# Query blocks of 256, 256, 512, 512, 512, a token-major second MLP product and a reordered prologue in a transformer block

## The chip, the cores and the metric

The kernel runs on one core of one Trainium2 chip. The metric is device time in microseconds (us) of one execution; the span of a profile, from its first to its last instruction, is about 2 us shorter (1296.0 us for an execution of 1298.07 us). TensorE, ScalarE, VectorE and GpSimd are the engines of that core; the profile calls them PE, ACT, DVE and POOL, and writes PEld for the weight loads of TensorE and SPq for DMA transfers issued by SyncE. All times compared below are of runs in the fast state.

## The reference

Shapes: 2048 tokens, width 1024, 32 heads of 32 that share one key and one value head, MLP width 3584, all bf16.

```python
mod = (silu(c) @ w_mod).reshape(1, 6, 1, -1)          # six vectors of 1024
sa, ca, ga, sb, cb, gb = ...
h = layernorm(x) * (1 + ca) + sa
x = x + ga * attention(h)        # q = h@wq (32 heads), k = h@wk, v = h@wv, softmax, @wo
h = layernorm(x) * (1 + cb) + sb
x = x + gb * (silu(h @ w1) * (h @ w3)) @ w2
```

## The kernel before

The program builds a graph of operations. A list scheduler inside the kernel file then lays out, before anything runs, one fixed instruction order for each engine, using durations that are written in the file. The traces below show instructions starting in that order: a VectorE product whose input is there at 716.4 us starts only when the sum ahead of it on VectorE is done, at 717.05 us. So a number such as `0.115` below changes no instruction at all; it changes only the order in which the instructions stand.

```python
def act_t(n):                       # what the scheduler believes a ScalarE instruction takes
    return n / 1200.0 + 0.115
...
    # in schedule(): the tie-break for VectorE, lower is earlier
            elif e == "dve":
                def key(c):
                    s, n = c
                    p = n.prio
                    if t - n.est > 4.0:
                        p -= 3
                    return (p, n.seq)
...
    BLOCKS = [(i * 512, 512) for i in range(NTB)]     # four blocks of 512 queries
    NU = 10                                           # ring of exponential buffers
    NTR = 5                                           # buffers of partial sums
...
    for bi, (q0, qn) in enumerate(BLOCKS):
        attention(q0, qn)      # scores -> exp -> value product, 8 head groups of 4 heads
        post(q0, qn)           # WO, residual, LN2, W1/W3, gate, W2: runs under the next block's attention
```

In a head group each of 16 key tiles takes one score step on TensorE (four heads side by side on 32-row tiles of the array), two exponentials of 128x1024 on ScalarE, and a share of a value product on TensorE. VectorE adds the exponentials in a tree, four tiles to one, and a product with ones turns the sums into denominators.

```python
                G.add("pe", smm, ..., prio=0, cls="S", mode="S", ...)        # score step
                for h in range(2):
                    G.add("act", ... ACT.Exp ..., dur=act_t(2 * npk * qn), prio=0, ...)
                ...
                    G.add("dve", ... TR[tr] = TR[tr] + U[u] ..., prio=3)       # tree sum, 128x2048
```

The MLP of a finished block fills TensorE between these steps. The gate of each of 28 feature tiles is one tanh on ScalarE and two products on VectorE; the first product frees the PSUM bank of the W1 result.

```python
            G.add("act", ... ACT.Tanh(TS <- PB[g1]) ..., dur=act_t(qn), prio=-1)
            G.add("dve", ... TT <- (TS + 1) * PB[g1] ..., prio=0)              # frees the bank of g1
            G.add("dve", ... HHT[ft] <- TT * PB[g3] ..., prio=0)
        ...
            # second product, feature-major: W2 tile stationary, 512 tokens moving
                return e.matmul(b[...], W2S[:, (d0 + j) % 2, fc, :], HHT[:, fc, 0:qn], ...)
            # then scale by the gate per feature, transpose back to tokens (PE), add to X (DVE)
```

The loads of the prologue, in the order of their issue: four token tiles, 4 MB of modulation weights, key and value weights, one eighth of WQ, four token tiles, the rest of WQ, WO, three modulation tiles, and only then the remaining token tiles.

Of the kernel before, what the change touches and what calls it, by code (L numbers as in the profile page):

```python
# [13 lines left out]
class Node:  # L14
    __slots__ = ("eng", "fn", "dur", "lat", "deps", "prio", "seq", "mode", "acq", "touch",
                 "start", "vis", "pos", "ndeps", "users", "need_inc", "cnt", "dsem", "dval", "nbytes", "est", "cls",
                 "sbanks")
# [8 lines left out]
class Dag:  # L26
# [12 lines left out]
    def add(self, eng, fn, reads=(), writes=(), dur=0.1, lat=0.1, prio=5, mode=None, cls=None,  # L39
            acq=None, groups=(), seq=None, dkey=None, nbytes=0, sbanks=()):  # L40
# [41 lines left out]
        for d in n.deps:  # L82
            d.users.append(n)
        n.dsem = n.dval = None
# [9 lines left out]
    def schedule(self, banks):  # L94
# [8 lines left out]
        for n in self.nodes:  # L103
            n.ndeps = len(n.deps)
            n.est = 0.0
            if n.ndeps == 0:
                ready[n.eng].append(n)
# [28 lines left out]
        while left:  # L136
# [85 lines left out]
            if n.dsem is not None:  # L222
                st = max(dma_free, s + 1.2)
                dma_free = st + n.nbytes / 230e3
                n.vis = dma_free + 0.8
            else:
                n.vis = s + d + n.lat
            for u in n.users:
                u.ndeps -= 1
                if not (e == "pe" and u.eng == "pe"):  # L230
                    u.est = max(u.est, n.vis + SEM_LAT)
# [75 lines left out]
def act_t(n):  # L307
    return n / 1200.0 + 0.115
# [9 lines left out]
def build(nc, x_in, wq_in, wk_in, wv_in, wo_in, w1_in, w3_in, w2_in, c_in, wmod_in, out, S, D, F):  # L318
# [9 lines left out]
    BLOCKS = [(i * 512, 512) for i in range(NTB)]  # L328
    NU = 10
    VB = 8  # L330
    R = 4
    NTR = 5
# [12 lines left out]
    WREG = sb("WREG", [P, 4 * 2048 + 2 * NF * P], BF16)  # L345
# [14 lines left out]
    NM = sb("NM", [P, NT], F32)  # L360
# [7 lines left out]
    O2B = HREG[:, o + 1024:o + 2048].rearrange("p (a s) -> p a s", a=2)  # L368
# [6 lines left out]
    U = UREG[:, 0:NU * 2048].rearrange("p (u g s) -> p u g s", u=NU, g=4)  # L375
    TR = UREG[:, NU * 2048:].rearrange("p (u g s) -> p u g s", u=NTR, g=4)
    WM01 = UREG[:, 0:NC * 2048].rearrange("p (c s) -> p c s", c=NC)
    assert (NU + NTR) * 2048 >= NC * 2048
    W1S = WREG[:, 0:2 * 2048].rearrange("p (a c f) -> p a c f", a=2, c=NC)
    W3S = WREG[:, 2 * 2048:4 * 2048].rearrange("p (a c f) -> p a c f", a=2, c=NC)  # L380
    W2S = WREG[:, 4 * 2048:].rearrange("p (a c f) -> p a c f", a=2, c=NF)
    WQ = WREG[:, 4 * 2048 - 2048:4 * 2048 - 2048 + NC * D].rearrange("p (c f) -> p c f", c=NC)
    WMS = WREG[:, 0:6144].rearrange("p (a c f) -> p a c f", a=3, c=4)
    GAB = WREG[:, 4 * 2048 - 2048 + NC * D:4 * 2048 - 2048 + NC * D + 1024]

    SP = nc.alloc_psum_tensor("SP", [P, 3, 2, 512], F32)
    PB = [nc.alloc_psum_tensor("PB%d" % i, [P, 512], F32)[:] for i in range(2)]
    PB += [SP[:, b, h, :] for b in range(3) for h in range(2)]
# [13 lines left out]
    def dma(fn, key, reads=(), writes=(), nbytes=0, prio=5, seq=None):  # L402
        return G.add("sp", fn, reads=reads, writes=writes, dur=0.06, dkey=key, nbytes=nbytes, prio=prio, seq=seq)
# [3 lines left out]
    def xload(t0, n):  # L407
        for t in range(t0, t0 + n):
            dma(lambda e, t=t: e.dma_start(X[:, t % NXS, :], x2[t * P:(t + 1) * P, :]),
                ("x", t % NXS), writes=[("X", t % NXS)], nbytes=P * D * 2)  # L410

    xload(0, 4)
    for k in range(NC):
# [7 lines left out]
    xload(4, 4)  # L421
    dma(lambda e: e.dma_start(WQ[:, :, P:D], wq_in[:, P:D].rearrange("(c p) f -> p c f", p=P)), "wq1",
        writes=[("WQ", 1)], nbytes=7 * P * D * 2)
    dma(lambda e: e.dma_start(WO[:], wo_in.rearrange("(c p) f -> p c f", p=P)), "wo", writes=["WO"], nbytes=D * D * 2)
# [41 lines left out]
    def ln_scale(t0, n):  # L466
        ks = [("MV", t0 + i) for i in range(n)]
        rk = [("RS", t0 + i) for i in range(n)]
        G.add("pool", lambda e: e.tensor_scalar(RS[:, t0:t0 + n], MV[:, t0:t0 + n, 1], EPS, None, ALU.add),
              reads=ks, writes=rk, dur=0.3)  # L470
        G.add("pool", lambda e: e.tensor_tensor(RS[:, t0:t0 + n], RS[:, t0:t0 + n], NHALF[:, 0:n], ALU.pow),
              reads=rk + ["NHALF"], writes=rk, dur=0.4)
        G.add("pool", lambda e: e.tensor_tensor(NM[:, t0:t0 + n], RS[:, t0:t0 + n], MV[:, t0:t0 + n, 0], ALU.mult),
              reads=rk + ks, writes=[("NM", t0 + i) for i in range(n)], dur=0.3)

    def ln_norm(t, q):
        s = t % NXS
        G.add("dve", lambda e: e.tensor_scalar(XN[:, q, :], X[:, s, :], RS[:, t:t + 1], NM[:, t:t + 1],
                                               ALU.mult, ALU.subtract),
              reads=[("X", s), ("RS", t), ("NM", t)], writes=[("XN", q)], dur=0.5, prio=2)  # L480

    def ln_transpose(nt, q0, dst, dkeys, fs, fm, engs, prio=5):
# [3 lines left out]
        for cb in range(NC // ncb):  # L486
            g = grp()
            for i in range(nt):
                def tr(e, i=i, g=g, cb=cb):
                    for h in range(ncb):  # L490
                        c = cb * ncb + h
                        r = e.transpose(PBH[g.bank][:, h * w + i * P:h * w + (i + 1) * P],
                                        XN[:, q0 + i, c * P:(c + 1) * P], IDENT[:])
                    return r
                G.add("pe", tr, reads=[("XN", q0 + i), "IDENT"], dur=ncb * 0.065, lat=0.2,
                      acq=g if i == 0 else None, groups=[(g, "w")], mode="F", prio=prio)
            for h in range(ncb):
                c = cb * ncb + h
                en = engs[cb % len(engs)]
                if en == "act":  # L500
# [4 lines left out]
                        dur=act_t(w) + 0.19, prio=2)  # L505
# [49 lines left out]
    for tb in range(NTB):  # L555
        for i in range(4):
            ln_stats(tb * 4 + i)
        ln_scale(tb * 4, 4)
        for i in range(4):
            ln_norm(tb * 4 + i, i)  # L560
        if tb + 2 < NTB:
            xload(tb * 4 + 8, 4)
        ln_transpose(4, 0, lambda c, tb=tb: HT[:, c, tb * 512:(tb + 1) * 512],
                     lambda c, tb=tb: [("HT", c, tb)], 0, 1, ("act", "dve") if tb == 0 else ("dve",))
        kv(tb)
        if tb == 0:
            qproj(0, 0)
    for f in range(1, NC):
# [5 lines left out]
    nwm = 0  # L574
    GAK = [("GAB",)]
    for h in range(2):
        g = grp()
        for kb in range(2):
            sl = nwm % 3
            nwm += 1  # L580
            dma(lambda e, kb=kb, h=h, sl=sl: e.dma_start(
                WMS[:, sl], wmod_in[kb * 512:(kb + 1) * 512, 2 * D + h * 512:2 * D + (h + 1) * 512]
                .rearrange("(c p) f -> p c f", p=P)), ("wms", sl), writes=wms(sl), nbytes=P * 2048 * 2)
# [314 lines left out]
```

## Time and profile before

The median is 1310.71 us in the runs made first, and 1311.88 us (1310.08 to 1313.36) over all four runs that the result compares (the first three among them).

| stage of the kernel before | from to (us) | what fills it |
|---|---|---|
| prologue and first head group | 0 to 91 | loads, LN1, projections; ScalarE partly idle |
| rest of block 0, two head groups of block 1 | 91 to 384 | attention and q projections, no MLP yet |
| rest of blocks 1 to 3 | 384 to 1107 | attention with MLP beneath it, mostly 33.0 us per head group |
| tail | 1107 to 1309 | TensorE alone: rest of an MLP, then the last MLP |

From the page of the kernel before: busy time of each engine, then 40 equal slices of the span with the busy share, or the granted TensorE clock, in tenths.

```profile
PE 1138.8 (87%) x8561; PEld 439.4 (34%) x8689; DVE 958.9 (73%) x1206; ACT 1015.3 (78%) x1142; POOL 17.1 (1%) x35
...
PE   5387896455779999999899999999999999999998
...
ACT  1368988999999999999979999998999998011100
...
PEclk8688996666889999999999999999999999999999
```

ScalarE has a hole near the start (the 3 in slice 2) and nothing to do in the last six slices. TensorE has slack up to slice 12, where the clock is also low; from there both are full. The average over the span hides that. Busy time of matmuls also overstates them: the Trainium skill, "Trainium Kernel Development and Optimization", section "Performance Expectations", calls it a bad metric because matmuls are pipelined. This trace agrees: one 512-column matmul counts 381 ns in the table of groups, while in a dense stream they start 216 ns apart. The counts and start-to-start times are used below.

Two groups of the page of before: busy time and mean of one in ns, then the idle time before them with its largest releaser.

```profile
L656 ACT ACTIVATE UREG<-SP 128x1024 bf16<-128x1024 f32 x1024 | 968.5, 1067 | 85.5 <-PE SP L646 65.9
...
L646 PE MATMUL SP<-QT,KT 32*128 32x512 bf16 x2048 | 215.4, 411 | 100.0 <-ACT UREG L656 93.9
```

Exponentials and score steps wait for each other. The waits of ScalarE between 29 and 1107 us in the kernel before (total us, times, longest us) are shown below. They include the first head group; from 91 us on the first line is 25.8 us, so ScalarE waits in these two ways for about 42 us in the thousand that follow:

```profile
ACT UREG L656 <- PE SP L646: 65.9, 50, 24.6
ACT UREG L656 <- PE PB L670: 16.6, 8, 3.9
```

One single wait is 24.6 us. The timeline of before (start, length, engine, line, operation, count, and in brackets the idle time before it with its releaser) shows where it comes from:

```profile
20.41 0.88 SPq L424 DMA_DIRECT2D WO<-in_A_wo_dram  x1
21.33 10.25 SPq L581 DMA_DIRECT2D WREG<-in_w_mod_dram  x3
31.70 39.35 SPq L409 DMA_DIRECT2D X<-in_A_x_dram  x16
...
50.47 1.28 DVE L461 BATCH_NORM_STATS2 ST<-X 128x6 f32<-128x512 bf16 x2
...
73.86 2.86 ACT L656 ACTIVATE UREG<-SP 128x1024 bf16<-128x1024 f32 x3 [24.64 <-PE SP L646]
```

The second half of the tokens is asked for at 31.7 us, behind WO and modulation weights; the statistics of the next token tiles can start only at 50.5 us; the exponentials that need their keys start at 73.9 us.

The windows of before: start, end and length, then busy time and instruction count of PE, PEld, DVE, ACT and POOL, granted clock, DMA share, GB/s.

```profile
29.00:91.00 62.00, 35.22 (x339) 17.68 (x339) 45.25 (x81) 29.68 (x32) 3.44 (x8) 0.72 0.36 124
205.00:385.00 180.00, 105.00 (x886) 29.41 (x891) 125.59 (x143) 165.37 (x179) 2.62 (x3) 0.70 0.10 23
1106.70:1155.20 48.50, 48.13 (x291) 23.10 (x295) 28.47 (x50) 1.02 (x2) 1.47 (x3) 1.00 0.48 94
1155.20:1252.20 97.00, 96.53 (x445) 44.08 (x453) 39.02 (x57) 16.72 (x28) 0.00 (x0) 1.00 0.54 151
1252.20:1308.60 56.40, 50.19 (x252) 23.41 (x255) 10.07 (x17) 0.00 (x0) 0.00 (x0) 0.98 0.56 117
```

The first head group needs 62 us with 29.7 us of ScalarE work. From 205 to 385 us TensorE is busy for 58% and the granted clock averages 0.70. The Trainium skill, "TensorE: Matmul & The Clock Gate", section "Part 1: The HAM clock gate", says that the array runs at half clock until it has been busy for a while and falls back when idle; a mean between a half and one in a stretch with idle gaps fits that, and the clock records of the two traces hold only the values 0.5 and 1.0. The last three windows are the tail: 48.5 us until the first W1 matmul of the last MLP, 97.0 us of W1 and W3, 56.4 us of W2 and the stores. TensorE is dense in it.

### The profile page before, as it was taken

What the parts mean: (1) busy time and instruction counts of PE and PEld (TensorE: products, weight loads), DVE (VectorE), ACT (ScalarE), POOL (GpSimd) and SP (SyncE); (2) the same over time, 40 slices, a digit from 0 to 9 for tenths busy, and PEclk for the clock granted to TensorE, in tenths of its full rate; (3) what the DMA queues carried; (4) which work ended last, traced back from release to release, by engine and by line L of the source; (5) the groups of instructions that cost most, each with busy time, mean ns of one, the idle gap of its engine ahead of it and who ended that gap; (6) DMA issues with size and microseconds to landing.
All of it is one profiled execution on the core that took longest, in us unless ns stands there. A gap on an engine that the chain in (4) does not pass through costs nothing.

```text
span 1308.6 us, 21172 instructions
## 1 busy us (share of the span) xinstructions
PE 1138.8 (87%) x8561; PEld 439.4 (34%) x8689; DVE 958.9 (73%) x1206; ACT 1015.3 (78%) x1142; POOL 17.1 (1%) x35
## 2 busy tenths in 40 slices
PE   5387896455779999999899999999999999999998
PEld 3133331111223333333333333333333333444443
DVE  5768786666798888778978887789888887643421
ACT  1368988999999999999979999998999998011100
POOL 1000000000000000000000000000000000000000
PEclk8688996666889999999999999999999999999999
DMA  9415104000003333342423333441533334375545
GB/s 313 151 41 178 33 1 110 12 1 1 1 1 97 98 97 97 94 85 57 120 78 94 95 94 94 93 77 29 157 97 98 97 97 85 77 175 147 160 83 118
DMA packets 253504, 118.93 MB, mean 91 GB/s; under 512 B 121312, under 2 KB 245216, under 8 KB 253408
## 3 DMA queue, kind: packets, MB, share of 16 engines
q1 hardware_dynamic: 253408, 117.59, 33.9%
q8 instruction: 68, 1.11, 0.4%
q14 instruction: 28, 0.23, 0.1%
HBM read 113.38 MB, written 4.19 MB: 90 GB/s over the span
## 4 chain that ended last, share of the span: by engine, by line
PE 58%; ACT 25%; DVE 9%; issue 6%; DMA 1%; POOL 1%; SPq 0%; DVEq 0%; ACTq 0%
ACT UREG L656 24%; PE PB L765 13%; PE PB L794 10%; PE PB L670 8%; PE SP L646 7%; PE SP L765 6%; PE SP L794 4%; PE PB L546 3%; PE PB L738 2%; ACT HREG L774 2%; DVE UREG L697 2%; DVE ST L461 1%; DVE UREG L702 1%; PE PB L712 1%; PE SP L738 1%
## 5 line engine op out<-in xcount | busy, mean ns | idle before, releaser
L656 ACT ACTIVATE UREG<-SP 128x1024 bf16<-128x1024 f32 x1024 | 968.5, 1067 | 85.5 <-PE SP L646 65.9
L765 PE MATMUL PB<-QT,WREG 128*128 128x512 bf16 x1397 | 343.3, 381 | 9.1 <-issue 6.4
L702 DVE TENSOR_TENSOR UREG<-UREG 128x2048 bf16<-128x2048 bf16 x256 | 310.5, 1213 | 38.4 <-ACT UREG L656 35.9
L646 PE MATMUL SP<-QT,KT 32*128 32x512 bf16 x2048 | 215.4, 411 | 100.0 <-ACT UREG L656 93.9
L697 DVE TENSOR_TENSOR UREG<-UREG 128x2048 bf16<-128x2048 bf16 x128 | 155.8, 1217 | 70.0 <-ACT UREG L656 69.9
L765 PEld LDWEIGHTS PB<-QT,WREG 128*128 128x128 bf16 x1456 | 125.7, 98 | 176.2 <-issue 52.3
L646 PEld LDWEIGHTS SP<-QT,KT 32*128 32x128 bf16 x2048 | 52.0, 92 | 313.4 <-ACT UREG L656 287.0
L794 PE MATMUL PB<-HREG,WREG 128*128 128x512 bf16 x612 | 153.3, 380 | 4.0 <-issue 2.5
L670 PE MATMUL PB<-UREG,V 128*32 128x512 bf16 x2016 | 142.9, 419 | 6.2 <-ACT UREG L656 5.8
L721 DVE RECIPROCAL DSB<-DSB 128x128 f32<-128x128 f32 x128 | 115.5, 928 | 0.1
L774 ACT ACTIVATE HREG<-SP 128x512 bf16<-128x512 f32 x28 | 16.7, 597 | 126.8 <-PE SP L765 123.9
L781 DVE TENSOR_TENSOR HREG<-HREG,PB 128x512 bf16<-128x512 bf16 x98 | 66.3, 676 | 19.6 <-PE PB L765 18.6
L794 PEld LDWEIGHTS PB<-HREG,WREG 128*128 128x128 bf16 x644 | 55.3, 98 | 73.5 <-issue 22.9
L765 PE MATMUL SP<-QT,WREG 128*128 128x512 bf16 x330 | 74.5, 379 | 0.3
L670 PEld LDWEIGHTS PB<-UREG,V 128*32 128x32 bf16 x2016 | 48.0, 101 | 78.9 <-issue 32.4
L776 DVE SCALAR_TENSOR_TENSOR HREG<-HREG,PB 128x512 bf16<-128x512 bf16 x84 | 57.5, 685 | 13.0 <-ACT HREG L774 9.9
L546 PE MATMUL PB<-HREG,WREG 128*128 128x512 bf16 x243 | 62.2, 389 | 1.7 <-DVE QT L549 0.8
L774 ACT ACTIVATE HREG<-PB 128x512 bf16<-128x512 f32 x84 | 56.5, 672 | 6.9 <-PE PB L765 6.8
L794 PE MATMUL SP<-HREG,WREG 128*128 128x512 bf16 x245 | 56.0, 379 | 0.4
L738 PE MATMUL PB<-WO,QT 128*128 128x512 bf16 x193 | 51.0, 389 | 2.9 <-DVE X L741 1.2
L776 DVE SCALAR_TENSOR_TENSOR HREG<-HREG,SP 128x512 bf16<-128x512 bf16 x28 | 19.3, 688 | 43.4 <-ACT HREG L774 43.4
L765 PEld LDWEIGHTS SP<-QT,WREG 128*128 128x128 bf16 x336 | 32.8, 98 | 39.4
(81 smaller groups left out, 547.9 us busy)
## 6 DMA issues: line engine op xcount, KB each, us to landing
WREG<-in_B_w_dram SPq DMA_DIRECT2D x112, 512.0 KB, 3.9
WREG<-in_B_w_dram SPq DMA_DIRECT2D x32, 896.0 KB, 5.9
X<-in_A_x_dram SPq DMA_DIRECT2D x32, 256.0 KB, 3.6
WREG<-in_w_mod_dram SPq DMA_DIRECT2D x16, 512.0 KB, 5.0
UREG<-in_w_mod_dram SPq DMA_DIRECT2D x8, 512.0 KB, 7.9
out_dram<-X SPq DMA_DIRECT2D x16, 256.0 KB, 2.6
WO<-in_A_wo_dram SPq DMA_DIRECT2D x1, 2048.0 KB, 14.6
WREG<-in_A_wq_dram SPq DMA_DIRECT2D x1, 1792.0 KB, 9.6
```

Of the source, the lines that this page charges most:

```text
L546: g = mm_group(NC, lambda e, b, c: e.matmul(b, WQ[:, c, f * P:(f + 1) * P], HT[:, c, sl], start=c == 0, stop=c == NC - 1), lambda c: [("WQ ...
L646: r = e.matmul(SP[:, bufs[gg // 2], gg % 2, j * qn:(j + 1) * qn], KT[32 * gg:32 * gg + 32, kt * P:(kt + 1) * P], QT[32 * gg:32 * gg + 32, ...
L656: G.add("act", lambda e, u=u, h=h, b=bufs[h]: e.activation(U[:, u, 2 * h:2 * h + 2, 0:npk * qn], SP[:, b, :, 0:npk * qn], ACT.Exp, scale=S ...
L670: r = e.matmul(PB[g.bank][32 * gg:32 * gg + 32, 0:qn], V[:, kt, :], U[:, pu, gg, j * qn:(j + 1) * qn], start=w0 + n == 0 and j == 0, stop= ...
L697: G.add("dve", lambda e, tr=tr, u=u, fu=first_u: e.tensor_tensor(TR[:, tr, :, 0:npk * qn], U[:, fu, :, 0:npk * qn], U[:, u, :, 0:npk * qn] ...
L702: G.add("dve", lambda e, tr=tr, u=u: e.tensor_tensor(TR[:, tr, :, 0:npk * qn], TR[:, tr, :, 0:npk * qn], U[:, u, :, 0:npk * qn], ALU.add), ...
L721: G.add("dve", lambda e, h=h: e.reciprocal(DSB[:, h * 128:(h + 1) * 128], DSB[:, h * 128:(h + 1) * 128]), reads=["DSB"], writes=[("DSBr", ...
L738: g = mm_group(NC, lambda e, b, f, t=t, h=h: e.matmul(b, QT[:, f, t * P:(t + 1) * P], WO[:, f, h * 512:(h + 1) * 512], start=f == 0, stop= ...
L765: return e.matmul(b[:, o:o + qn], w13[w][:, sl, c, sub * P:(sub + 1) * P], QT[:, c, q0:q0 + qn], start=c == 0, stop=c == NC - 1)
L774: G.add("act", lambda e, g=g1: e.activation(TS[:, 0:qn], PB[g.bank][:, 0:qn], ACT.Tanh, scale=0.5), writes=["TS"] + alias("TS"), groups=[( ...
L776: G.add("dve", lambda e, g=g1: e.scalar_tensor_tensor(TT[:, 0:qn], TS[:, 0:qn], 1.0, PB[g.bank][:, 0:qn], ALU.add, ALU.mult), reads=["TS"] ...
L794: return e.matmul(b[:, j * qn:(j + 1) * qn], W2S[:, (d0 + j) % 2, fc, :], HHT[:, fc, 0:qn], start=fc == 0, stop=fc == NF - 1)
```

## The change

It has six parts. Tokens load before everything that can wait, and the second group of tokens gets its own buffer for normalised rows. The first block is split in two, so that MLP work exists earlier. In blocks after the first, two of eight head groups get their denominators straight from the exponentials on TensorE, without VectorE sums. LN2 is scaled per token tile, not per block. The second product is turned: activations stationary, 256 columns of W2 moving, so its result is token-major and needs no transpose; its weights share one ring with W1 and W3. Last, several durations that the scheduler believes are changed; the one of ScalarE comes nearer to the measured spacing.

```diff
 def act_t(n):
-    return n / 1200.0 + 0.115
+    return n / 1200.0 + 0.057
...
-                dma_free = st + n.nbytes / 230e3
+                dma_free = st + n.nbytes / 300e3
...
-    BLOCKS = [(i * 512, 512) for i in range(NTB)]
+    BLOCKS = [(0, 256), (256, 256), (512, 512), (1024, 512), (1536, 512)]
+    FIVE = 9          # an alternative PSUM layout, not used
+    NDIR = 2
...
-    xload(0, 4)
+    xload(0, 8)
...                                   # WQ rest, WO moved behind all token loads
-    xload(4, 4)
+    dma(... WQ[:, :, P:D] ..., after=xl)
+    wo_load = dma(... WO ..., after=xl)
...                                   # modulation weights behind WO
-                ("wms", sl), writes=wms(sl), nbytes=P * 2048 * 2)
+                ("wms", sl), writes=wms(sl), nbytes=P * 2048 * 2, after=[wo_load])
...                                   # denominators
+            direct = f < ndirect
...
+                    for kind, dst in (("V", ASB), ("D", DSB))[0:2 if direct else 1]:
+                        g = batch(pend, kind, qn)      # "D": ONES instead of V as the weights
...                                   # LN2
-        ln_scale(t0, nt)
-        for i in range(nt):
-            ln_norm(t0 + i, i)
+            ln_scale(t, 1)            # inside the loop over the tiles
+            ln_norm(t, i)
...                                   # second product
-                return e.matmul(b[:, j * qn:(j + 1) * qn], W2S[:, (d0 + j) % 2, fc, :], HHT[:, fc, 0:qn], ...)
+                    return e.matmul(b[:, j * 256:(j + 1) * 256], HHT[:, fc, (i0 + j) * P:(i0 + j + 1) * P],
+                                    W2S[:, r, fc, :], ...)
...                                   # gate as a broadcast row GBB; transposes gone
```

Cut from this diff: the parts that only rename or re-index, a cheaper form of the normalisation, ScalarE's share in normalising the second group of tokens, a higher priority for the reciprocals of the last head group, and three more durations of the scheduler (normalisation, reciprocal, ScalarE's scaling). Of the durations only the 0.057 is tested by itself below.

> **What bounds the kernel now.** ScalarE and TensorE together, in a long middle stage. The group of exponentials (1024 of 128x1024) follows at 0.905 us start to start (timeline, back to back), so it needs 927 us at least; 84 tanh under attention add about 0.48 us each, 40 us. By windows, ScalarE is 95 to 99% busy from 131 us to 1107 us. From about 385 us TensorE has no slack either: every head group takes 33.0 us, filled by 512-column matmuls 0.216 us apart, score steps, and about 0.1 us at each change between them. Three stretches lie outside this balance:
>
> 1. Prologue. The first exponential starts at 29 us, then ScalarE idles, longest 24.6 us before 73.9 us (waits view). The timeline shows why: the loads of tokens 1024 to 1535, issued at 31.7 us, queue behind 5 MB of weights; their statistics start at 50 us. The first head group takes 62 us, not 33.
> 2. 205 to 385 us: attention of block 0 with no MLP to fill TensorE; granted clock 0.63 to 0.69 (windows view).
> 3. Tail: the last exponential starts at 1107 us; TensorE is then dense to 1302 us. About 165 us is the last block's own work (736 matmuls at 0.216 us, plus transposes); about 30 us is the previous block's unfinished second product (its matmuls end at 1155 us).
>
> **What the change does.**
> - Prologue: tokens 512 to 1023 load first, the rest of the weights wait for all token loads, and the second group normalises into its own buffer. The 24.6 us gap should mostly close. The modulation weights come about 3 us later (1 MB more before them), and VectorE, about 80% busy from 65 us on, limits the catch-up. Estimate: 15 to 22 us gained.
> - A first block of 256 lets TensorE start MLP work near 190 us rather than 383 us. But the posts done under attention stay 1536 queries, so an MLP-less stretch returns in the second half of block 2. Saturated stretches stay 512 long, so the leftover at the end stays near 30 us. Estimate: 0 to 8 us gained. Weights stream five times, not four.
> - Direct denominators for two of eight head groups: about 100 us of VectorE tree sums go (466 us x 7/8 x 1/4); TensorE pays 12 more steps of about 0.22 us each, about 5 us per 512-block. VectorE is freed where the LN2 work competes. Net: 0 to 5 us gained.
> - Second product token-major: twice the matmuls, 256 columns. By the Trainium skill, "TensorE: Matmul & The Clock Gate", section "Back-to-back issue gap", N/2.4 + 2.5 ns gives 109 ns; this trace agrees at 512 columns (216 ns) and at 128 (transposes 56 ns apart, each with its own weight load). So no loss. It removes 32 transposes per 512-block, about 2 us. Its weights now share the ring with W1/W3, exposing an estimated 3 us of load in the tail.
> - LN2 per tile: a few us of the 1107 to 1155 us stretch, which leftover work already covers. Estimate 0 to 5 us.
>
> **Prediction.** 1279 us, 8 in 10 between 1248 and 1300. Faster by over 2%: 0.58; within 2%: 0.39; slower: 0.03.
>
> **Signs.** First head groups dense by about 35 to 45 us, no gap over 10 us; last exponential near 1080 us; tail still 190 to 200 us, opening with leftover second product; first W1 matmuls near 190 to 200 us; a low-clock stretch inside block 2; second-product matmuls 0.109 us apart; VectorE share near 67%.
>
> **What would make it wrong.** Faster: the leftover vanishes, or VectorE relief tightens the 33 us groups. Slower: 256-column phases starved by weight loads[...], weight loads not hidden at 256 columns, or VectorE eating the prologue gain.

## The result, and the profile after

The changed kernel has a median of 1298.65 us (1298.07 to 1299.73, four runs) against 1311.88 us. The ratio is 0.9901, with a 95% interval of 0.9884 to 0.9918. A ratio here is always the mean time of one kernel's fast runs over that of the other's of the same rounds, so it is not quite the ratio of the medians quoted. The result is correct. So the change gains 1.0%; the forecast was 2.4%, and its largest single chance was on faster by over 2%.

The page after, the same lines:

```profile
PE 1177.5 (91%) x11393; PEld 583.5 (45%) x11393; DVE 877.7 (68%) x1223; ACT 1011.0 (78%) x1174; POOL 20.8 (2%) x51
...
PE   5698998899898889868999999999999999999998
...
ACT  1499999999899999989999999989999996011100
...
PEclk9898999999899999868999999999999999999999
```

The hole near the start is gone and the low-clock stretch is short (the 8 and 6 in slices 17 and 18). VectorE lost 81 us of work. Groups of the page after, exponentials and the second product:

```profile
L715 ACT ACTIVATE UREG<-SP 128x1024 bf16<-128x1024 f32 x1024 | 969.6, 1172 | 60.6 <-PE PB L659 32.1
...
L838 PE MATMUL PB<-WREG,HREG 128*128 128x256 bf16 x1232 | 152.8, 273 | 2.7 <-DVE HREG L843 1.8
```

The waits of ScalarE after, between 80 and 1088 us:

```profile
ACT UREG L715 <- PE PB L659: 32.1, 22, 2.6
ACT UREG L715 <- PE SP L704: 11.0, 12, 1.8
```

This is the first surprise. In the kernel before, ScalarE waited behind a value product (line 670) for 16.6 us in 8 waits; now it waits behind one (line 659) for 32.1 us in 22 waits. Its waits for score steps fell in return, from 25.8 us to 11.0, so outside the prologue the two together are about 43 us, as before. The prologue after, from the timeline:

```profile
1.18 3.67 SPq L416 DMA_DIRECT2D X<-in_A_x_dram  x8
...
20.12 4.72 SPq L416 DMA_DIRECT2D X<-in_A_x_dram  x8
...
25.37 0.85 SPq L579 DMA_DIRECT2D WO<-in_A_wo_dram  x1
...
61.86 2.85 ACT L715 ACTIVATE UREG<-SP 128x1024 bf16<-128x1024 f32 x3 [6.47 <-PE SP L704]
```

The token loads are issued by 25 us and go ahead of WQ and WO. A head group of 256 queries has 16 exponentials, one of 512 has 32, so the same work is compared by counting 32 exponentials: two head groups after, one before. The longest gap of ScalarE in them is now 6.5 us. The first exponential comes 9 us later (38.05 against 29.18 us), but 32 are through at 80.7 us and not at 91.3. Windows after:

```profile
38.00:81.00 43.00, 37.00 (x478) 18.24 (x477) 34.93 (x58) 29.86 (x33) 1.27 (x2) 0.94 0.30 97
540.00:619.00 79.00, 58.22 (x521) 18.97 (x522) 44.77 (x65) 70.33 (x77) 3.17 (x8) 0.78 0.09 27
1087.60:1144.40 56.80, 56.80 (x498) 43.55 (x496) 30.76 (x53) 1.35 (x2) 3.17 (x8) 1.00 0.34 94
1144.40:1242.50 98.10, 96.87 (x450) 43.74 (x448) 39.62 (x58) 16.72 (x28) 0.00 (x0) 1.00 0.57 164
1242.50:1296.00 53.50, 49.08 (x448) 43.74 (x448) 8.93 (x16) 0.00 (x0) 0.00 (x0) 1.00 0.45 124
```

The last exponential starts 19.1 us earlier (1087.6 against 1106.7), but the tail behind it is 6.5 us longer (208.4 against 201.9). Its first part, the work left over under the last attention, grew by 8.3 us (56.8 against 48.5, with TensorE dense in both); W1 and W3 take 1.1 us more and the end 2.9 us less. What was won on ScalarE is partly paid back there.

Where the time goes can be counted for TensorE: its work is the matmuls counted in the trace (missing records filled from their weight loads) times their start-to-start spacing; the rest of a stretch is waiting and changes between kinds of matmul. Between the starts of the exponentials of query 0, 512, 1024 and 1536 and the last one, this rest is 157, 59, 45 and 39 us before, and 76, 78, 63 and 47 us after. The early MLP removes about 81 us of it from the first quarter, and about 45 us come back in the other three. Where the exponentials of query 512 begin, the changed kernel is 23.9 us ahead (296.7 against 320.6 us); at the last exponential it is 19.1 us ahead, at the end 12.6.

### The profile page after: what moved, and what is told of

Read it like the earlier page. It is cut to its first block, busy times and chain, and to the rows that moved or that the text cites. A ratio compares the mean times of both kernels' runs of the same rounds, so it can differ in the third digit from the quotient of the medians.

```text
span 1296.0 us, 26693 instructions
## 1 busy us (share of the span) xinstructions
PE 1177.5 (91%) x11393; PEld 583.5 (45%) x11393; DVE 877.7 (68%) x1223; ACT 1011.0 (78%) x1174; POOL 20.8 (2%) x51
## 4 chain that ended last, share of the span: by engine, by line
PE 43%; ACT 41%; issue 6%; DVE 6%; DMA 3%; SPq 1%; ACTq 0%; DVEq 0%
ACT UREG L715 38%; PE PB L809 9%; PE PB L838 7%; PE SP L704 5%; PE SP L809 5%; PE PB L659 5%; PE SP L838 5%; ACT HREG L818 3%; PE PB L786 2%; DMA WREG<-in_B_w_dram 1%; DVE UREG L744 1%; PE PB L554 1%; PE PB L760 1%; DMA WREG<-in_w_mod_dram 1%; DMA UREG<-in_w_mod_dram 1%
## 5 line engine op out<-in xcount | busy, mean ns | idle before, releaser
L715 ACT ACTIVATE UREG<-SP 128x1024 bf16<-128x1024 f32 x1024 | 969.6, 1172 | 60.6 <-PE PB L659 32.1
L809 PE MATMUL PB<-QT,WREG 128*128 128x512 bf16 (+1 forms) x1904 | 361.7, 331 | 6.8 <-DVE DSB L766 2.0
L749 DVE TENSOR_TENSOR UREG<-UREG 128x2048 bf16<-128x2048 bf16 x200 | 243.2, 1216 | 31.8 <-ACT UREG L715 29.2
L704 PE MATMUL SP<-QT,KT 32*128 32x512 bf16 (+1 forms) x2560 | 207.5, 348 | 57.8 <-ACT UREG L715 44.2
L744 DVE TENSOR_TENSOR UREG<-UREG 128x2048 bf16<-128x2048 bf16 x100 | 121.5, 1215 | 87.3 <-ACT UREG L715 86.7
L838 PE MATMUL PB<-WREG,HREG 128*128 128x256 bf16 x1232 | 152.8, 273 | 2.7 <-DVE HREG L843 1.8
L659 PE MATMUL PB<-UREG,V 128*32 128x512 bf16 (+1 forms) x2528 | 138.1, 353 | 10.2 <-DVE HREG L820 4.6
L838 PEld LDWEIGHTS PB<-WREG,HREG 128*128 128x128 bf16 x1232 | 113.1, 98 | 40.3 <-issue 24.8
L818 ACT ACTIVATE HREG<-PB 128x512 bf16<-128x512 f32 (+1 forms) x126 | 82.2, 652 | 46.9 <-PE PB L809 42.7
L820 DVE SCALAR_TENSOR_TENSOR HREG<-HREG,PB 128x512 bf16<-128x512 bf16 (+1 forms) x126 | 71.0, 563 | 45.8 <-ACT HREG L818 37.7
L659 PEld LDWEIGHTS PB<-UREG,V 128*32 128x32 bf16 x2528 | 59.2, 99 | 69.9 <-issue 25.8
L554 PE MATMUL PB<-HREG,WREG 128*128 128x512 bf16 x256 | 66.2, 384 | 1.2 <-DVE QT L557 1.1
L838 PE MATMUL SP<-WREG,HREG 128*128 128x256 bf16 x560 | 62.8, 273 | 1.3 <-DMA WREG<-in_B_w_dram 1.3
L809 PEld LDWEIGHTS SP<-QT,WREG 128*128 128x128 bf16 x336 | 32.9, 98 | 39.4
```

The lines of the kernel that those rows point to most:

```text
L554: g = mm_group(NC, lambda e, b, c: e.matmul(b, WQ[:, c, f * P:(f + 1) * P], HT[:, c, sl], start=c == 0, stop=c == NC - 1), lambda c: [("WQ ...
L659: r = e.matmul(PB[g.bank][32 * gg:32 * gg + 32, 0:qn], V[:, kt, :] if kind == "V" else ONES[:], U[:, pu, (gg * npk + j) * qn:(gg * npk + j ...
L704: r = e.matmul(SP[:, b, o:o + w], KT[32 * gg:32 * gg + 32, kts[j] * P:(kts[j] + 1) * P], QT[32 * gg:32 * gg + 32, f, q0 + qo:q0 + qo + w], ...
L715: G.add("act", lambda e, u=u, h0=h0, n=n, b0=b0, nb=nb, wb=wb: e.activation(U[:, u, h0 * W:(h0 + n) * W].rearrange("p (b w) -> p b w", b=n ...
L744: G.add("dve", lambda e, tr=tr, u=u, fu=first_u: e.tensor_tensor(TR[:, tr, 0:4 * W], U[:, fu, 0:4 * W], U[:, u, 0:4 * W], ALU.add), reads= ...
L749: G.add("dve", lambda e, tr=tr, u=u: e.tensor_tensor(TR[:, tr, 0:4 * W], TR[:, tr, 0:4 * W], U[:, u, 0:4 * W], ALU.add), reads=[("TR", tr) ...
```

## The experiments

The theory as it took shape: the load order gives the whole gain; from the first MLP on TensorE is the limit, so time won on ScalarE alone returns in the tail; and the changed constants of the scheduler gave an instruction order with more waits, which took back what the other parts could have won. The rivals: the added TensorE work (denominators, 256-column products) took it back; or the block split did not pay; or LN2 and the second product did. The quoted expectations were written as the theories then stood. Every run was correct and in the fast state. Intervals of 95% are given in brackets.

| kernel | median us | ratio to before | last exponential, end (us) |
|---|---|---|---|
| the change | 1298.65 | 0.9901 [0.9884, 0.9918] | 1087.6, 1296.0 |
| b_loads | 1291.80 | 0.9846 [0.9824, 0.9868] | 1088.6, 1290.5 |
| a_loads | 1317.09 | 1.0033 [1.0019, 1.0047] | 1107.1, 1315.6 |
| b_blocks | 1306.93 | 0.9978 [0.9941, 1.0015] | 1106.0, 1304.0 |
| b_loads_blocks | 1293.61 | 0.9870 [0.9856, 0.9883] | 1096.2, 1294.1 |
| a_4x512 | 1313.21 | 1.0006 [0.9991, 1.0021] | 1094.6, 1310.3 |
| a_nu11 | 1296.38 | 0.9882 [0.9867, 0.9897] | 1056.0, 1296.6 |
| a_ndir0 | 1297.40 | 0.9884 [0.9869, 0.9898] | 1093.4, 1295.2 |
| a_w2old | 1304.23 | 0.9940 [0.9924, 0.9957] | 1087.6, 1301.7 |
| a_ln4 | 1293.52 | 0.9861 [0.9844, 0.9878] | 1082.5, 1291.5 |
| b_act057 | 1339.01 | 1.0205 [1.0182, 1.0228] | 1136.5, 1336.9 |
| a_act115 | 1291.58 | 0.9840 [0.9817, 0.9863] | 1093.9, 1289.6 |
| a_act095 | 1282.59 | 0.9780 [0.9766, 0.9793] | 1085.0, 1281.2 |
| a_swap5 | 1296.23 | 0.9875 [0.9860, 0.9890] | 1086.2, 1294.9 |
| a_act10_nd0 | 1277.71 | 0.9746 [0.9731, 0.9760] | 1080.4, 1277.5 |
| a_split6 | 1266.91 | 0.9663 [0.9650, 0.9677] | 1072.4, 1263.3 |

Names that start with b_ are the kernel before with one part of the change; those with a_ are the changed kernel with one part undone or altered.

### The load order, alone and undone

b_loads is the kernel before with the new order of the loads and nothing else:

```diff
-    xload(0, 4)
+    xload(0, 8)
...
-    xload(4, 4)
-    dma(... "wq1" ...)
-    dma(... "wo" ...)
...   # after the loop over token groups
+    dma(... "wq1" ..., after=xl)
+    wo_load = dma(... "wo" ..., after=xl)
...
-  ("wms", sl), ...)
+  ("wms", sl), ..., after=[wo_load])
```

> The kernel before with the new order of the prologue's loads alone (eight token tiles first; the rest of the q weights, the output weights and the gate weights behind all token loads). Theory L (the load order is the one part of the change that gains, and the gain passes through to the end): head group 0 ends 15 to 20 us earlier, every later head group takes what it took (33.0 us with MLP), tail near 202 us, total 1292 to 1297 us, no slower than the full change. Rival M (the gain comes from the split first block and the others, and the load order's gain alone is eaten because a TensorE-bound middle stage gives it back): total within 5 us of before.

It took 1291.80 us, 1.5% less than before, and less than the whole change. Its timeline at the first head group has one line where the kernel before had a 24.6 us hole:

```profile
45.83 34.67 ACT L662 ACTIVATE UREG<-SP 128x1024 bf16<-128x1024 f32 x37 [3.77 <-PE SP L652]
```

The group ends at 73.6 us (before: 91.3). Every later head group takes what it took before within 0.3 us (one took 0.7 us less), and the tail is 201.9 us in both. So the whole 18 us of the prologue reaches the end: all that follows hangs on the first head group.

a_loads is the reverse, the changed kernel with the old order of the loads.

> The changed kernel with the loads of before in the prologue, all else as changed. The load order gained 20 us on the kernel before (ratio 0.985). If it passes through here too: 12 to 20 us slower than the changed kernel, 1310 to 1318 us, so the whole rest of the change is worth nothing net on the kernel before; head group 0 takes about 63 us, the later head groups unchanged. If TensorE's saturated stage swallows it: under 6 us slower.

It took 1317.09 us, slower than the change by 18 us and slower than the kernel before (ratio 1.0033). Its first 32 exponentials are through at 99.2 us, not at 80.7. The two runs agree on the size, 18 to 20 us, and they say more: **without the load order, the rest of the change is worth nothing or a little less than nothing.** The question is thus not where a prologue gain went, but why the other five parts give nothing.

### The block split

b_blocks is the kernel before with the new list of blocks; b_loads_blocks adds the load order to it; a_4x512 is the changed kernel with four blocks of 512.

```diff
-    BLOCKS = [(i * 512, 512) for i in range(NTB)]
+    BLOCKS = [(0, 256), (256, 256), (512, 512), (1024, 512), (1536, 512)]     # b_blocks, b_loads_blocks
```

```diff
-    BLOCKS = [(0, 256), (256, 256), (512, 512), (1024, 512), (1536, 512)]
+    BLOCKS = [(0, 512), (512, 512), (1024, 512), (1536, 512)]                 # a_4x512
```

> The kernel before with the five blocks alone. Theory L: no gain, 1305 to 1316 us: MLP starts near 220 to 240 us instead of 383 us, but a stretch without MLP comes back in the second half of block 2, and with one head group of 16 key-tile steps of 256 queries the prologue has less work to overlap. Rival M: 1290 to 1298 us.

> The kernel before with the new load order and the five blocks, nothing else. If the two gains add (20 us and 3 us alone): 1286 to 1292 us. If the split spoils the prologue (a head group of 256 queries gives ScalarE half the work while the keys are being made; in the runs so far head group 0 ended near 81 us with the split and near 72 to 74 us without): head group 0 ends at 80 us or later, and the total is 1294 to 1304 us, slower than the loads alone.

> The changed kernel with four blocks of 512 again (direct denominators then in blocks 1 to 3). Prediction's estimate (the split gains 0 to 8 us): 1298 to 1306 us. Theory T: the early MLP start fills about 45 us of idle TensorE in the changed kernel, so without it 1302 to 1312 us, with first W1 matmuls near 370 us, although head group 0 should end about 7 us earlier than in the changed kernel (it did so in the run with the loads alone). Rival: as the kernel before showed no gain from the split (ratio 0.998), none here either: within 4 us of 1298.

In the kernel before, the split brings the first W1 matmul from 383.5 to 228.3 us, and the time stays the same: the interval of 0.9978 includes 1. On top of the load order it gives nothing either, 1293.61 against 1291.80 us. In the changed kernel, though, taking the split away costs 1.1%: 1313.21 us, with about 307 us of waiting and kind changes on TensorE, counted as above over the whole span, instead of 289. So the split has no fixed worth. It lets TensorE start the MLP early, but an early start helps only if the later stages leave no gaps in return. In the kernel before they do: with b_blocks the waiting and kind changes of the four quarters, counted as above, are 98, 88, 60 and 45 us instead of 157, 59, 45 and 39, so 59 us leave the first and 51 come back in the others. Without the split, a_4x512 has 126, 62, 47 and 48. In the changed kernel without the split, the rest of the change even loses the whole load-order gain, although its first head group ends at 71.9 us, 19 us before that of the kernel before.

### What the limit is once MLP work is there

a_nu11 gives the ring of exponentials an eleventh buffer, taken from the partial sums.

```diff
-    NU = 10
+    NU = 11
...
-    NTR = 5
+    NTR = 4
```

> The changed kernel with 11 instead of 10 buffers for exponentials (and 4 instead of 5 for the tree sums, same memory): ScalarE may run one key-tile step further ahead before a value product must free a buffer. Theory T: ScalarE's waits of 2.1 us per head group go and the last exponential comes 20 to 40 us earlier (1048 to 1068 us), but the total falls by no more than 6 us (1292 to 1300 us), because the tail grows by almost as much: TensorE's work is not done sooner. Rival S (the waits of ScalarE are what costs): the total falls by most of what the last exponential gains, 1265 to 1285 us.

This run separates the two engines best. Its waits of ScalarE between 80 and 1057 us, the ScalarE row of its page, and the window behind its last exponential:

```profile
...
ACT UREG L715 <- PE PB L659: 7.8, 7, 2.4
```

```profile
ACT  1499999999999999999999999999999960011100
```

```profile
1056.00:1144.90 88.90, 88.90 (x694) 62.74 (x693) 40.10 (x69) 4.76 (x8) 3.16 (x8) 1.00 0.46 125
```

The wait behind the value product fell from 32.1 to 7.8 us, ScalarE is full from end to end, and the last exponential starts at 1056.0 us, 31.6 us earlier than in the changed kernel. The end did not move: 1296.6 us. All 31.6 us came back as TensorE work after the last exponential, 88.9 us with no idle time where the changed kernel has 56.8. TensorE's waiting and kind changes are about 289 us in both. So from the first MLP on the sum of TensorE's work, kind changes and waits decides, and a wait of ScalarE costs nothing unless it makes TensorE idle. The chain of waits does not show this: on the page of the changed kernel it gives ScalarE 41% and TensorE 43%. The run also took a buffer from VectorE's sums and redrew the order; what a larger ring alone would do was not tested.

### Denominators, second product and LN2, each undone

a_ndir0 sets `NDIR = 0`. a_w2old puts the old feature-major second product, its transposes and its gate per feature back, on the shared ring of weights. a_ln4 scales LN2 per block again.

```diff
-    NDIR = 2
+    NDIR = 0          # a_ndir0
```

```diff
-                    return e.matmul(b[:, j * 256:(j + 1) * 256], HHT[:, fc, (i0 + j) * P:(i0 + j + 1) * P], W2S[:, r, fc, :], ...)
+                return e.matmul(b[:, j * qn:(j + 1) * qn], W2S[:, (dt // 2) % 2, fc, (dt % 2) * P:(dt % 2 + 1) * P],
+                                HHT[:, fc, 0:qn], ...)      # a_w2old; gate per feature and transposes follow as before
```

```diff
-            ln_scale(t, 1)
-            ln_norm(t, i)
+        ln_scale(t0, nt)                # a_ln4
+        for i in range(nt):
+            ln_norm(t0 + i, i)
```

> The changed kernel with no direct denominators (VectorE sums all of them). Theory T (TensorE's time is what the total is made of from the first MLP on, so its 19 us of extra denominator matmuls cost time and the relieved VectorE gains little): matmul work falls by about 19 us, VectorE's share returns from 68% toward 75%, the tail after the last exponential shortens from 208 us toward 200, total 1286 to 1295 us. Rival V (the relief of VectorE is worth its price, that is why the direct form was taken for the first two head groups): total at 1298 us or above, with head groups right after a block boundary longer than in the changed kernel.

> The changed kernel with the second MLP product feature-major again (512 columns, evictions scaled per partition, transposes back), on the shared weight ring. Prediction's estimate (token-major gains about 2 us per block at no matmul cost): 1300 to 1308 us. Rival W (256-column matmuls or the new evictions cost more than the transposes did): faster than 1298 by over 3 us.

> The changed kernel with LN2's scale computed once per block again (the third operation of before stays away). Prediction's estimate for the per-tile form is 0 to 5 us gained, so 1298 to 1303 us. Theory O: the order is redrawn as well, by chance in either direction; leftover work covers the latency, so the part itself is worth under 3 us: 1293 to 1301 us.

Without direct denominators the time is 1297.40 us, the same. The mechanism is as costed: TensorE's work, counted as above, falls by 18 us (about 1000 to 982). But its waiting and kind changes rise by 17 us (289 to 306). Two stretches of 32 exponentials just after block boundaries show where some of it sits: they take 39.0 and 38.3 us instead of 31.1 and 32.1, with 8 us of idle ScalarE in each. VectorE has the tree sums, the old block's last reciprocals and LN2 to do there. The waits of the second stretch (592 to 631 us) in the trace of a_ndir0:

```profile
PE PB L500 <- DVE XN L486: 5.4, 2, 4.9
ACT UREG L715 <- PE PB L659: 7.0, 1, 7.0
```

TensorE waits for the rows that LN2 normalises on VectorE, and ScalarE for the value product behind them. That the sums are what delays VectorE was not tested by itself. The direct denominators buy about 17 us of relief for 18 us of TensorE work. So the rival that added TensorE work ate the gain is right about the size of that work and, for the denominators in this order, wrong about the result.

The old second product costs 5.6 us (ratio 0.9940 against 0.9901). The token-major form is a gain, as expected from the matmul spacing: 0.109 us for 256 columns against 0.216 us for 512. LN2 per block is 5 us faster than LN2 per tile. This does not show that LN2 per tile is bad, because any edit also makes the scheduler draw a new order; the two can't be told apart by this run, and the next experiments show that a redrawn order alone can be worth more than that.

### The order alone

These runs change no instruction, only the constant by which the scheduler lays out the order.

```diff
-    return n / 1200.0 + 0.115
+    return n / 1200.0 + 0.057          # b_act057, on the kernel before
```

```diff
-    return n / 1200.0 + 0.057
+    return n / 1200.0 + 0.115          # a_act115, on the changed kernel; 0.095 in a_act095
```

> The kernel before with the scheduler's cost of a ScalarE instruction changed from 0.115 to 0.057 us per instruction, alone; no instruction changes, only the static order on each engine. Theory O (the nearer-to-truth cost makes an order without slack, in which a VectorE tree sum stands ahead of the gate product and so of a PSUM bank that the next value product needs): head groups with MLP rise from 33.0 to 34 to 36 us, total 1318 to 1332 us, slower than before. Rival (the constant is harmless or helps, as it is closer to the 0.905 us pitch): within 5 us of before or faster.

> The changed kernel with the old scheduler cost (0.115) restored, nothing else; only the static order differs. Theory O: head groups with MLP of the 512-blocks fall from 34.5 us toward 33 us, the 2.1 us idle of ScalarE per group goes, total 1280 to 1292 us, so 5 to 18 us faster than the changed kernel (1298 us). Rival W (the changed kernel's late part is slow because of added TensorE work, whatever the order): total within 4 us of 1298.

> The changed kernel with the scheduler's cost of a ScalarE instruction at 0.095 us (0.057 in the change, 0.115 before), order only. Theory O (0.057 is an unlucky order; the design of the change is worth more than it shows): total 1278 to 1288 us, that is 10 to 20 us under the changed kernel's 1298 us, with a tail under 202 us or head groups under 34 us. Rival W (order is worth at most the 7 us that the cost 0.115 returned): 1289 to 1298 us.

The kernel before gets 27 us slower from the new constant alone (1339.01 us, ratio 1.0205): its last 16 head groups average 34.4 us (31.9 to 36.4) instead of 32.9. The changed kernel gets 7 us faster with the old constant (1291.58 us) and 16 us faster with 0.095 (1282.59 us). The constant 0.057 is the better description of the exponentials: 1024/1200 + 0.057 is 0.910 us, and the trace has them 0.905 us apart. Among the orders tried it is also the worst choice. The order that it leads to has more waiting: on the kernel before, TensorE's waiting and kind changes rise from about 318 to 346 us with the same work. Two constants were tried on the kernel before and three on the changed one; whether the kernel before also has an order better than its own was not tested.

How the order costs TensorE time can be seen at one place. Two head groups under MLP work hold 57.0 us of matmuls and about 70 changes between kinds of matmul in both kernels. A change costs about 0.1 us in the trace (0.312 to 0.327 us to the next start instead of 0.216), which agrees with the Trainium skill, "TensorEngine Tiling (Array Packing)", section "Key Properties", that switching the tiling mode drains the array. They took 66.0 us before and 69.1 us after. From the timeline of the changed kernel:

```profile
715.51 0.86 ACT L818 ACTIVATE HREG<-PB 128x512 bf16<-128x512 f32 x1
715.91 1.23 DVE L744 TENSOR_TENSOR UREG<-UREG 128x2048 bf16<-128x2048 bf16 x1 [0.43 <-ACT UREG L715]
717.05 0.68 DVE L820 SCALAR_TENSOR_TENSOR HREG<-HREG,PB 128x512 bf16<-128x512 bf16 x1
...
717.79 1.91 PE L659 MATMUL PB<-UREG,V 128*32 128x512 bf16 x32 [0.76 <-DVE HREG L820]
718.45 2.86 ACT L715 ACTIVATE UREG<-SP 128x1024 bf16<-128x1024 f32 x3 [2.09 <-PE PB L659]
```

The tanh ends at 716.4. The gate product that reads it (line 820) stands on VectorE behind a tree sum of 1.23 us, starts at 717.05 and ends at 717.7. Only then is its PSUM bank free, and the value product takes that bank. TensorE waits 0.76 us, and the exponentials behind it 2.09 us. The same place in the kernel before:

```profile
734.88 0.76 ACT L774 ACTIVATE HREG<-PB 128x512 bf16<-128x512 f32 x1
...
735.82 0.68 DVE L776 SCALAR_TENSOR_TENSOR HREG<-HREG,PB 128x512 bf16<-128x512 bf16 x1
...
736.94 1.91 PE L670 MATMUL PB<-UREG,V 128*32 128x512 bf16 x32
737.51 1.22 DVE L697 TENSOR_TENSOR UREG<-UREG 128x2048 bf16<-128x2048 bf16 x1 [0.30 <-ACT UREG L656]
```

Here the gate product comes first and the tree sum later; TensorE shows no wait before the value product (a score step, cut here, stands between, and had waited 0.20 us for ScalarE).

a_swap5 repairs this pattern wherever it occurs. After the order is drawn, a tree sum is swapped with the gate product behind it when the scheduler expects that product to be ready within 0.5 us of the sum's start.

```diff
+        o = order["dve"]
+        for i in range(len(o) - 1):
+            if o[i].prio == 3 and o[i + 1].prio == 0 and o[i + 1].est - o[i].start < 0.5:
+                o[i], o[i + 1] = o[i + 1], o[i]
+        for i, n in enumerate(o):
+            n.pos = i
         self.order = order
```

> The changed kernel, its static order kept but for VectorE: where a tree sum stands directly ahead of a gate product that becomes ready within 0.5 us of the sum's start, the two are swapped. Theory O in its fine form (that sum holds the gate product, it holds a PSUM bank, the bank holds the value product on TensorE): head groups with MLP of the last blocks fall from 34.5 to about 33.8 us, total 2 to 5 us under the changed kernel. Rival (the sum's place does not matter to TensorE): head groups stay at 34.5 us, total within 1 us. The 0.095 and 0.100 orders gained 16 to 20 us, so in any case most of the gain of those orders is then not this one swap.

From the timeline of a_swap5, the same place:

```profile
...
718.22 0.69 DVE L826 SCALAR_TENSOR_TENSOR HREG<-HREG,PB 128x512 bf16<-128x512 bf16 x1 [0.92 <-ACT HREG L824]
718.83 1.22 DVE L750 TENSOR_TENSOR UREG<-UREG 128x2048 bf16<-128x2048 bf16 x1
718.97 1.91 PE L665 MATMUL PB<-UREG,V 128*32 128x512 bf16 x32
```

The gate product now starts right after the tanh (which starts at 717.33 us), and the sum follows. The value product starts 1.64 us after the start of the tanh, not 2.28. The head groups that took 34.5 us take 33.8. The whole gained about 3 us (ratio 0.9875 against 0.9901; the intervals touch, but the difference is just larger than both together allow), while a_act095 gained 16. So this pair is a real cause and a small one. Nor is it a measure of how good an order is: summed over the trace, gate products start 21.4 us late in the changed kernel (34 of 140 by more than 0.1 us after their tanh), 6.8 us in a_swap5, and 37.2 us in a_act095, which is faster than both. What else makes one order better than another was not settled.

### A version that beats both

Two edits that the runs above suggested were tried together: a constant between the two, with VectorE doing all sums again (a_act10_nd0), and then more of the early blocks split (a_split6). The values were chosen offline, by a replay that is not on record; the chip then decided.

```diff
-    return n / 1200.0 + 0.057
+    return n / 1200.0 + 0.1
...
-    BLOCKS = [(0, 256), (256, 256), (512, 512), (1024, 512), (1536, 512)]
+    BLOCKS = [(0, 256), (256, 256), (512, 256), (768, 256), (1024, 512), (1536, 512)]   # a_split6 only
-    NDIR = 2
+    NDIR = 0
```

> The changed kernel at cost 0.100 and without direct denominators. If the direct form is neutral in any order (it was at 0.057: 1297.4 against 1298.7): within 4 us of the run at 0.095. If the direct form costs TensorE time once the order no longer wastes it: 5 to 12 us faster than that run, 1270 to 1280 us.

> As the run at cost 0.100 without direct denominators, with blocks of 256, 256, 256, 256, 512, 512. Theory T (TensorE idle before the saturated stage is what the split removes): another 3 to 8 us off, about 1270 us, since the stretch without MLP gets no longer and one more 512-block no longer feeds a leftover. Rival (weights stream once more, 22 MB, and two more block boundaries cost): no faster than that run.

a_act10_nd0 takes 1277.71 us. Most of its head groups under MLP work take 32.7 us, and two of them 65.5 us instead of 69.1 with the same matmul time inside. Over three head groups (666 to 764 us) the waits of TensorE in its trace are the first line below; those of the changed kernel (661 to 765 us) are in the second fence.

```profile
PE PB L809 <- issue: 1.4, 9, 0.2
```

```profile
PE PB L659 <- DVE HREG L820: 2.3, 3, 0.8
PE PB L760 <- DVE ASB L730: 1.1, 2, 0.5
...
```

In the changed kernel TensorE waits for VectorE there; in this version it does not. Direct denominators were neutral under one order and are not needed under another; no run has the constant 0.1 with `NDIR = 2`, so how much of the 5 us between this run and a_act095 is theirs is open.

a_split6 takes 1266.91 us, ratio 0.9663: 45 us less than before, 32 us less than the change. Its last exponential starts at 1072.4 us and its tail is 190.9 us, the shortest of all runs here. This split, too, redraws the order, so its 11 us are not shown to be the split's own.

## Why the prediction was right or wrong

The time, 1298.65 us, lies within the range of 1248 to 1300, at its edge. The class with the highest chance, faster by over 2%, was wrong.

**Right: the prologue.** "15 to 22 us gained" is 20 us when done alone and 18 us when undone. The sign "no gap over 10 us" held, with 6.5 us as the longest. "First head groups dense by about 35 to 45 us" did not, if it is read as a time: ScalarE still waits for 6.5 us before 61.9 us.

**Right: the second product.** "0.109 us apart" was measured. "No loss" is a gain of 5.6 us, and the "estimated 3 us of load in the tail" is one wait of 1.3 us for weights. The Trainium skill's formula, "TensorE: Matmul & The Clock Gate", section "Back-to-back issue gap", N/2.4 + 2.5 ns, which the page gives for the isolated case, yields 216, 109 and 56 ns for 512, 256 and 128 columns; the trace has just these three in dense streams.

**Right in mechanism: direct denominators.** TensorE pays 18 us for 1792 queries, as "about 5 us per 512-block" adds up to. VectorE's share is 68%, forecast "near 67%". The net of "0 to 5 us" is about nothing: a_ndir0 is the same within its interval.

**Wrong in size: the split.** "0 to 8 us" was 15 us in the changed kernel, and in the one before not clear of zero. The term has no value of its own. The sign "first W1 matmuls near 190 to 200 us" missed too: 223.2 us, because q projections, which come first in the order, run until 213 us. The low-clock stretch is there (clock 0.78 from 540 to 619 us), but only its first 20 us lie inside block 2 (0.63 from 540 to 560 us); the rest falls into block 3.

**Wrong or unsettled: LN2 per tile.** "0 to 5 us" gained; undoing it gained 5 us, mixed with a redrawn order.

**The step that failed** is the one that says "Saturated stretches stay 512 long, so the leftover at the end stays near 30 us", with the balance of 33.0 us per head group that it carries over from the kernel before. The leftover grew: the second product of the block before the last has 133 matmuls of 512 columns (28.7 us) left at the last exponential before, and 351 of 256 columns (38.3 us) after, which makes the first part of the tail 8.3 us longer (56.8 against 48.5 us). The head groups did not get shorter either: the last 16 average 33.05 us against 32.9. The repeated ones in the middle of a block take 34.5 us, most others 29 to 34. So more than half of the idle time that the early start removed returned later, about 45 of 81 us on TensorE by the count above; b_blocks shows that the split alone, with the order that it draws, does this.

Beside this stands a term that the sum did not have at all. The change redraws the static order, and the new constant of ScalarE draws it for the worse. Measured alone, that term is 27 us lost on the kernel before, and 7 to 16 us that can be had back on the changed one by choosing another constant; at 0.095 it takes 1282.59 us, close to the 1279 forecast. The forecast was 33 us of gain and 13 were measured, so this term has the size of 7 to 16 of the 20 us that are missing, though other orders of the kernel before were not searched. The forecast does not mention the changed durations; they add no instruction.

The second half of the failed step is that a saturated stage was taken as limited by both engines. a_nu11 shows that ScalarE is not part of that limit: it can gain 31.6 us and the end stays. So the gains that were booked because the last exponential would come early ("near 1080 us"; it came at 1087.6) were worth less than booked; they return in the tail unless TensorE's own idle time falls. Over the whole span, TensorE's count has about 983 us of work before and 1000 after, and 318 and 289 us of waiting and kind changes. Waiting fell by 29 us, work rose by 17, and 12 us remain. The denominators alone add 18 us of work; the other parts about cancel.

What stays open: which pairs of instructions carry the remaining cost of the order (one was shown, worth about 3 us). The single effects do not add up either. Undoing the parts one at a time gives 18 us for the loads, 15 for the split and 6 for the second product in favour of the change, and 1, 5 and 7 against it for denominators, LN2 and the constant: a balance of about 25 us in its favour, where it gained 13. Each removal also redraws the order.

## What to carry to other kernels

When a program's order is drawn statically from estimated durations, a changed estimate is a change of the program, and it needs its own line in the forecast and its own run: here it was worth 27 us on one kernel and up to 16 on the other, as much as any part of the change but the load order. Where two engines look full, give one of them slack (a deeper ring of buffers will do) and see whether the end moves; if it does not, count the other engine's work and idle time, and book gains only there. A prologue on which everything hangs passes its gain on in full, so load first what the first long stage waits for.

## What the Trainium skill lacked or had wrong

- "TensorE: Matmul & The Clock Gate", section "Back-to-back issue gap", gives a sustained spacing in streams of weight load and matmul of about 81 ns at 128 columns and 131 ns at 512, and says that N/2.4 + 2.5 ns holds for the isolated case. Here the dense streams, each matmul with its own weight load, run at 56 ns (128, transposes), 109 ns (256) and 216 ns (512): the formula holds in the stream, and the two sustained figures do not.
- "ScalarE: Activation LUTs", section "What ACT_TABLE_LOAD costs", gives 186 ns plus 0.833 ns per element and an overlap of about 93 ns back to back; an estimate from that is 946 ns for 1024 elements and 520 ns for 512. The traces have exponentials of 128x1024 starting 905 ns apart, and a tanh of 128x512 between them takes 478 ns more, both about 41 ns less.
- "TensorEngine Tiling (Array Packing)", section "Key Properties", says that a mode switch drains the array and gives no time there. Here a change between kinds of matmul cost about 0.1 us, and there are about 35 in each head group under MLP work.
- No page says how much the order of instructions on an in-order engine can matter when PSUM banks tie the engines together. Here the same instructions in another order took 27 us more (1339.01 against 1311.9 us), and one VectorE sum of 1.23 us ahead of the product that frees a bank held TensorE for 0.76 us.
